# P times V in eight tensor tiles of 64 keys by 32 columns, with the halves added on GpSimd

## The chip, the cores and the metric

The kernel runs on one core of one Trainium2 chip. A core has a tensor engine (PE, with its weight loads shown as PEld), a vector engine (DVE), a scalar engine (ACT), GpSimd (POOL), and SyncE (SP), whose queue issues most of the transfers. Matrix products go into PSUM banks; the scalar and vector engines read them from there, and GpSimd works on tiles in SBUF. The metric is the device time in microseconds, the median of several executions. The profile is of one execution more.

## The reference

There are 2048 tokens of width 512, and two branches on them, mixed by a gate per token:

```
g = sigmoid((x * gate_w).sum(-1))
a = attention(x)          # 32 heads of 16, causal, window 256, softmax, then @ wo
b = mlp(layernorm(x'))    # 512 -> 1792, gelu, -> 512
out = g * a + (1 - g) * b
```

In the attention a query sees itself and the 255 keys before it:

```
mask = (i_q - i_k >= 0) & (i_q - i_k < 256)
p = softmax(where(mask, q @ k.T / 4, -1e9))
o = p @ v
```

Everything is float32 in memory.

## The kernel before, in words

There are three stages. The first makes q, k and v (lines 292, 307, 342) and the layer norm. The second holds the attention and the first MLP product side by side. The third makes the second MLP product (line 860) and the output projection (line 836).

The change touches the second stage. Its work is cut into units, and a string, `ORDER`, gives the order in which the tensor engine does them, one letter a unit:

- `S` (`s_pair`, line 368): scores of 128 queries against up to 384 keys for two heads, each head on one half of the array's rows. The vector engine takes the row maxima out of the banks (line 373).
- `T` (`st_pair`, line 412): the same scores transposed, 128 keys (block `kb`) by up to 384 queries, for two heads: `e` = 0 uses rows 0 to 63, `e` = 1 rows 64 to 113. The scalar engine takes the exponential into the tile `pts[p, kb]` (line 414), and GpSimd clears what the window excludes with one or two selects (line 416). `pts[p, kb]` holds four heads, and its 384 columns are the queries from the block's own start on.
- `f` (`fill`, line 635): one step of 24 of an MLP unit, two matmuls of 512 columns, one on each half of the rows. A unit keeps a bank pair over its 24 steps; its two banks are then copied out by the scalar engine and stored to `hp`.
- `P` (`pv`, line 431): P times V for a group `p` of four heads and 256 queries, `j`. There are 8 groups and 8 `j`, 64 units. The four heads go to the four column tiles of 32 columns (`tile_position=(0, 32 * h)`). For each head the unit has a matmul over 128 keys for each key block that its queries reach: blocks 2j - 1, 2j - 2, 2j, 2j + 1 with 256, 128, 256 and 128 queries (the two last alone where j = 0). The sums stand in one bank, 128 x 256. The scalar engine copies them (line 138) into half of an SBUF tile `acc[p]`; in the last stretch, when no S unit is left but T units are, the vector engine does (line 438). After an odd `j` the tile is stored to `osc`: by SP, one block later (line 444), or by GpSimd's own queue when all T units are out (line 446).

Scores, MLP and P times V share four bank pairs, b0 to b3, in a ring: each unit takes the one used longest ago, and an MLP unit takes one out of the ring while it runs. A bank pair can be written again when its reader is done.

A block is a T unit with `pr` = 0: `block` first calls `tick`, which runs what was put off by `after(k, ...)` until k blocks later; then it issues transfers of q and k stacks (`load_stacks`). So what stands in `after(1, ...)` is issued at the next block, ahead of that block's exponentials and selects in every engine's queue.

SBUF tiles of 128 x 512 named `t` come from a pool of nine in this stage. They serve the MLP copies (`out_half`), the raw w1 and early w2 weights, and `acc`. The early w2 loads begin at block 5 of the last group, and `attn_sums(0)`, at its block 11, is the first reader of `osc`. When the T units are out, `first_h` does the gelu and the split (line 702) of the first two tiles for the third stage, whose first matmuls (line 860) follow the last P units.

Line 138 is the helper `copy`, which is an activation on the scalar engine; line 135 is a helper that subtracts.

Of the kernel before, what the change touches and what calls it, by code (L numbers as in the profile page):

```python
# [17 lines left out]
ALU = mybir.AluOpType  # L18
# [14 lines left out]
VW = 17  # L33
# [38 lines left out]
def gated_mix_kernel(ctx, tc: tile.TileContext, xt, x2, wqk, wv, wo, xa, gw, w1, w2, b1, b2, out):  # L72
    nc = tc.nc
    dve, act, pool, pe, sp = nc.vector, nc.scalar, nc.gpsimd, nc.tensor, nc.sync
# [18 lines left out]
    def get(key, tag, bufs, shape, dt=F32):  # L93
        return left[key].tile(list(shape), dt, name=nm(tag), tag=tag, bufs=bufs)
# [3 lines left out]
    def t2(dt=F32, shape=(128, 512), tag="t"):  # L98
        return get("work", tag, BUFS.get(tag) or nt[0], shape, dt)
# [13 lines left out]
    def ps(tag, shape=(128, 512)):  # L113
        key, bufs = banks[tag]
        return left[key].tile(list(shape), F32, name=nm("ps_" + tag), tag=tag, bufs=bufs)
# [3 lines left out]
    def two():  # L119
        if not ring:  # L120
            return ps("x", (128, 2, 512))
        ring.append(ring.pop(0))
        return ps(ring[-1], (128, 2, 512))
# [13 lines left out]
    def copy(dst, src):  # L137
        act.activation(dst, src, AF.Copy)  # L138
# [3 lines left out]
    done = set()  # L142

    def after(k, fn):
        todo.setdefault(step[0] + k, []).append(fn)
# [10 lines left out]
    osc = dram.tile([8, 128, S], F32, name="osc")  # L156
# [9 lines left out]
    vs = get("ring", "v", 1, (128, NB, VR))  # L166
# [230 lines left out]
    pts, acc = {}, {}  # L397
# [21 lines left out]
    def flush():  # L419
        while late:  # L420
            late.pop(0)()

    def pv(p, j, last):
        flush()
        a = two()[:, 0]
        parts = ((-1, 0, 128, 256), (-2, 0, 256, 128), (0, 0, 0, 256), (1, 128, 0, 128))[0 if j else 2:]
        for n, (d, at, fr, w) in enumerate(parts):
            kb = 2 * j + d
            for h in range(4):
                v = (4 * p + h) * VW  # L430
                pe.matmul(a[32 * h:32 * h + 32, at:at + w], vs[:, kb, v:v + 32], pts[p, kb][:, h, fr:fr + w],  # L431
                          start=n == 0, stop=n == len(parts) - 1, skip_group_check=True, tile_position=(0, 32 * h))
        if j % 2 == 0:
            acc[p] = t2()
        s = acc[p]
        o = j % 2 * 256
        if last:
            dve.tensor_copy(s[:, o:o + 256], a[:, :256])
        else:
            copy(s[:, o:o + 256], a[:, :256])  # L440
        if j % 2:
            to = osc[p, :, (j - 1) * 256:(j + 1) * 256]
            if lt:
                after(1, lambda: sp.dma_start(to, s))
            else:
                pool.dma_start(to, s)
            done.add(("o", p, j))

    def load_consts():
        sp.dma_start(gws, view(gw, [0, 128], [1, D]))  # L450
# [275 lines left out]
    def fill():  # L726
        if cur[0] is None:
            assert {("w", *jobs[0][:2]), ("y", jobs[0][2], KT - 1)} <= done
            cur[0] = mlp1_unit(*jobs.pop(0))
        if next(cur[0], 0) == 0:  # L730
            cur[0] = None

    def block(p, kb):
        tick()
        if kb % 2 == 0:
            if kb and p + 1 < 8:
                load_stacks(p + 1, kb * 128 - 256, 256)
            if not kb and p:
                load_stacks(p, S - 256, 256)
        if p in (0, 2, 4) and kb % 2:  # L740
            double(p // 2 + 1, kb // 4, kb // 2 % 2)
        if p == 7 and kb == EB:
            early_w2()
        if p == 7 and kb == 12:
            early.extend(load_h(0, f) for f in range(2))
        if p == 7 and kb == 11:
            attn_sums(0)

    early = []
    lt = [(p, kb, pr) for p in range(8) for kb in range(NB) for pr in range(2)]  # L750
    ls = [(p, qb, pr) for p in range(8) for qb in range(NB) for pr in range(2)][2 * (NB - LAG):]
    lp = [(p, j) for p in range(8) for j in range(NB // 2)]

    def run(order):
        for a in order:
            flush()
            if a == "T":
                p, kb, pr = lt.pop(0)
                if not pr:
                    block(p, kb)  # L760
                st_pair(p, kb, pr)
                if not lt:
                    first_h()
            elif a == "S":
                s_pair(*ls.pop(0))
            elif a == "P":
                a = lp.pop(0)
                if a:
                    pv(*a, lt and not ls)
            else:  # L770
                fill()

    def first_h():
        t = spare[0]
        for f, (gelu, parts) in enumerate(early):
            gelu()
            parts((t[:, f * 2 * C:f * 2 * C + C], t[:, f * 2 * C + C:f * 2 * C + 2 * C]))

    run(ORDER)
    flush()  # L780
    run("P")
    settle()
    close_pool("work")
# [92 lines left out]
    for n in range(len(seq)):  # L876
# [10 lines left out]
        k = n + EH if n < 8 else n + 8  # L887
# [56 lines left out]
```

## Time and profile before

| | |
|---|---|
| median of 3 executions | 689.37 us (689.32 to 692.36) |
| the profiled execution | 688.0 us, of which the profile's span is 686.3 |
| tensor engine busy | 677.0 us, 99% |
| vector, scalar, GpSimd busy | 478.7, 365.4, 278.2 us |
| first and last matmul of line 431 | 156.8 and 482.9 us |
| matmuls on line 431, as the profile counts them | 1920 |

In the profile's lines, `out<-in` names the tiles written and read, `x` a count, and after the bar stand the busy time in us, the mean ns of one, and the idle time of the engine before them with what ended it. Tensor tiles are given as rows*columns. In the chain and in the timeline the first two numbers are the start and the length in us. In the waits the numbers are the total in us, the times and the longest. A float32 matmul of line 431 is run as two passes, each with its weight load, and each pass is a record.

### The profile page before, as it was taken

How to read it: one execution, taken by the hardware profiler on the slowest of the kernel's cores; microseconds unless marked ns; L12 is line 12 of the kernel's file. 1: busy time of each engine (PE TensorE's matmuls, PEld its weight loads, DVE VectorE, ACT ScalarE, POOL GpSimd, SP SyncE). 2: the span in 40 equal slices, each digit the busy share in tenths (PEclk: the TensorE clock that was granted, in tenths of full speed). 3: DMA queues.
4: the chain of work that ended last, by engine and by line, in shares of the span. 5: the costliest groups of instructions: out<-in, count | busy, mean ns of one | idle time of the engine just before them, and what ended most of it. 6: DMA issues, size and time to landing. Idle time of an engine off the chain costs nothing.

```text
span 686.3 us, 16344 instructions
## 1 busy us (share of the span) xinstructions
PE 677.0 (99%) x5738; PEld 542.4 (79%) x5738; DVE 478.7 (70%) x1491; ACT 365.4 (53%) x584; POOL 278.2 (41%) x553
## 2 busy tenths in 40 slices
PE   9999999999999999999999999999998999999997
PEld 7877777877777888787888777787877888888886
DVE  5378967797887877767868778885675654736723
ACT  5343223367776777677767678778633324214221
POOL 7210029735474655566546458558230020200300
PEclk9999999999999999999999999999999999999999
DMA  8899886886667577665685755736992551922901
GB/s 268 276 309 325 285 258 220 282 242 196 211 213 220 160 223 237 212 204 185 188 245 190 208 163 168 222 99 194 342 270 87 187 171 50 275 82 88 238 1 61
DMA packets 91590, 138.21 MB, mean 201 GB/s; under 512 B 15124, under 2 KB 38868, under 8 KB 91380
## 3 DMA queue, kind: packets, MB, share of 16 engines
q1 hardware_dynamic: 90468, 135.46, 63.0%
q8 instruction: 45, 0.74, 0.5%
q0 software_dynamic: 320, 1.05, 0.4%
q10 hardware_dynamic: 720, 0.66, 0.3%
q14 instruction: 37, 0.30, 0.1%
HBM read 81.80 MB, written 54.28 MB: 198 GB/s over the span
## 4 chain that ended last, share of the span: by engine, by line
PE 88%; DMA 8%; DVE 2%; ACT 1%; issue 1%; SPq 1%; POOL 0%; DVEq 0%; POOLq 0%; ACTq 0%
PE ps_b L635 23%; PE ps_a L860 18%; PE ps_b L431 12%; PE ps_d L307 10%; PE ps_b L412 7%; PE ps_b L368 6%; PE ps_o L836 6%; PE ps_d L342 4%; DMA or<-rd 2%; DMA t<-in_xa 2%; DMA b2s<-in_b 1%; DMA e<-hp 1%; PE ps_d L292 1%; DMA qk<-t 1%; DMA t<-in_wqk 1%; PE ps_x L368 1%
## 5 line engine op out<-in xcount | busy, mean ns | idle before, releaser
L373 DVE CUSTOM_DVE_ANT_0 scr<-ps_b,wide 128x384 bf16<-128x384 f32 (+1 forms) x472 | 227.6, 530 | 63.5 <-PE ps_b L368 61.6
L635 PE MATMUL ps_b<-x,w 64*128 64x512 f32 x1344 | 208.7, 392 | 0.7 <-DVE t L135 0.7
L416 POOL TENSOR_SCALAR_AFFINE_SELECT p<-p 128x256 f32<-128x256 f32 x368 | 140.7, 414 | 127.0 <-ACT p L414 125.6
L414 ACT ACTIVATE p<-ps_b 128x768 f32<-128x768 f32 x192 | 146.6, 795 | 30.5 <-PE ps_b L412 23.1
L860 PE MATMUL ps_a<-x,h 128*128 128x512 f32 x648 | 149.0, 389 | 0.0
L860 PEld LDWEIGHTS ps_a<-x,h 128*128 128x128 f32 x648 | 121.7, 188 | 25.2
L635 PEld LDWEIGHTS ps_b<-x,w 64*128 64x128 f32 x1344 | 128.7, 186 | 10.4 <-DVE t L135 1.1
L412 PE MATMUL ps_b<-q,k 64*128 64x384 f32 (+5 forms) x512 | 90.2, 345 | 0.2 <-DVE mx L373 0.2
L368 PE MATMUL ps_b<-k,q 62*128 62x384 f32 (+2 forms) x472 | 82.1, 336 | 0.0
L818 POOL TENSOR_TENSOR or<-or,or 128x512 f32<-128x512 f32 x16 | 22.9, 1430 | 144.2 <-DMA or<-rd 135.0
L138 ACT ACTIVATE t<-ps_b 128x256 f32<-128x256 f32 (+1 forms) x116 | 52.8, 487 | 43.5 <-PE ps_b L431 35.2
L431 PE MATMUL ps_b<-p,v 128*32 128x256 f32 (+1 forms) x1472 | 71.8, 330 | 0.0
L412 PEld LDWEIGHTS ps_b<-q,k 64*128 64x128 f32 (+1 forms) x512 | 49.2, 184 | 16.6 <-DVE mx L373 3.6
L431 PEld LDWEIGHTS ps_b<-p,v 128*32 128x32 f32 x1472 | 42.3, 110 | 23.1 <-issue 2.8
L368 PEld LDWEIGHTS ps_b<-k,q 62*128 62x128 f32 (+1 forms) x472 | 46.5, 185 | 10.1 <-issue 1.4
L416 POOL TENSOR_SCALAR_AFFINE_SELECT xq<-xq 128x256 f32<-128x256 f32 x112 | 44.3, 422 | 22.0 <-ACT xq L414 21.8
L414 ACT ACTIVATE xq<-ps_b 128x768 f32<-128x768 f32 (+1 forms) x64 | 44.2, 706 | 14.1 <-PE ps_b L412 11.7
L839 DVE SCALAR_TENSOR_TENSOR us<-b2s,g,us 128x512 f32<-128x512 f32 x16 | 12.0, 752 | 56.0 <-ACT us L838 56.0
L836 PE MATMUL ps_o<-wo,a 128*128 128x512 f32 x192 | 46.0, 390 | 2.7 <-ACT a L138 1.8
L138 ACT ACTIVATE t<-ps_d 128x512 fp32r<-128x512 f32 x32 | 19.0, 596 | 52.8 <-PE ps_d L307 45.8
L135 DVE TENSOR_TENSOR h<-e,h 128x512 fp32r<-128x512 f32 x54 | 41.0, 759 | 5.3 <-DVE h L702 0.5
L836 PEld LDWEIGHTS ps_o<-wo,a 128*128 128x128 f32 x192 | 36.0, 188 | 10.9 <-ACT a L138 2.2
(92 smaller groups left out, 754.5 us busy)
## 6 DMA issues: line engine op xcount, KB each, us to landing
qk<-t SPq DMA_DIRECT2D x72, 256.0 KB
e<-hp SPq DMA_DIRECT2D x55, 256.0 KB
hp<-t SPq DMA_DIRECT2D x54, 256.0 KB
k<-qk SPq DMA_DIRECT2D x112, 98.0 KB
q<-qk SPq DMA_DIRECT2D x112, 98.0 KB
osc<-t SPq DMA_DIRECT2D x30, 256.0 KB
w<-w SPq DMA_DIRECT2D x28, 256.0 KB
qk<-qk SPq DMA_DIRECT2D x24, 256.0 KB
```

Of the source, the lines that this page charges most:

```text
L135: eng.tensor_tensor(out=lo, in0=src, in1=f32(hi), op=ALU.subtract)
L138: act.activation(dst, src, AF.Copy)
L307: pe.matmul(o, a[:, dt * 128:(dt + 1) * 128], b[:, dt * C:(dt + 1) * C], start=n == 0, stop=n == 11)
L368: pe.matmul(o[:, e, :n], qs[pr][r:k, qb * 128:qb * 128 + 128], ks[pr][r:k, t0:t0 + n], start=True, stop=True)
L373: dve.tensor_tensor_reduce(out=sc[:, :n], in0=o[:, e, :n], in1=wide[:, 384 - n:], scale=1.0, scalar=NEG, op0=ALU.add, op1=ALU.max, accum_o ...
L412: pe.matmul(o[:, e, :w], ks[pr][r:k, kb * 128:kb * 128 + 128], qs[pr][r:k, kb * 128:kb * 128 + w], start=True, stop=True)
L414: act.activation(pt[:, :, :w], o[:, :, :w], AF.Exp, scale=0.25)
L416: pool.affine_select(out=pt[:, :, a:a + 128], in_=pt[:, :, a:a + 128], pattern=[[0, 2], [sgn, 128]], base=b, channel_multiplier=-sgn, comp ...
L431: pe.matmul(a[32 * h:32 * h + 32, at:at + w], vs[:, kb, v:v + 32], pts[p, kb][:, h, fr:fr + w], start=n == 0, stop=n == len(parts) - 1, sk ...
L635: pe.matmul(o[:, e], w[kt // 4][r:r + 64, k, m:m + 128], y[r:r + 64, a:a + C], start=n == 0, stop=n == 23)
L836: pe.matmul(a, hl[g][x][:, b * 128:b * 128 + 128], wos[g][:, k], start=n == 0, stop=n == 11)
L860: pe.matmul(accs[c][b], x[:, b * 128:(b + 1) * 128], w, start=f == 0 and n == 0, stop=f == FT - 1 and n == 2)
```

## The change

A `P` unit now works on eight tiles of 64 keys by 32 columns. The rows of a key block are taken as two halves, `r` = 0 and 1, and each half has a bank of its own in the bank pair. `parts[r]` lists, for each half, the key block (`d`), the first query column it writes (`at`) and how many (`w`). A half moves only the queries that one of its 64 keys reaches: the first half 256, 192, 128 and 64 queries of blocks 2j, 2j - 1, 2j + 1 and 2j - 2, the second half 256, 192, 128 and 64 of blocks 2j - 1, 2j, 2j - 2 and 2j + 1. For j = 0 the first half moves 256 and 128, the second 256 and 64.

The scalar engine copies both banks, 2 x 256 columns, into a `t` tile `u` of its own, always; GpSimd adds the two halves of `u` into `acc[p]`. The add is put off by one block, and the store by one more, while T units are left; after that both are issued at once.

```diff
-    def pv(p, j, last):
+    def pv(p, j):
         flush()
-        a = two()[:, 0]
-        parts = ((-1, 0, 128, 256), (-2, 0, 256, 128), (0, 0, 0, 256), (1, 128, 0, 128))[0 if j else 2:]
-        for n, (d, at, fr, w) in enumerate(parts):
-            kb = 2 * j + d
-            for h in range(4):
-                v = (4 * p + h) * VW
-                pe.matmul(a[32 * h:32 * h + 32, at:at + w], vs[:, kb, v:v + 32], pts[p, kb][:, h, fr:fr + w],
-                          start=n == 0, stop=n == len(parts) - 1, skip_group_check=True, tile_position=(0, 32 * h))
+        a = two()
+        if j:
+            parts = ((0, 0, 256), (-1, 0, 192), (1, 128, 128), (-2, 0, 64)), ((-1, 0, 256), (0, 64, 192), (-2, 0, 128), (1, 192, 64))
+        else:
+            parts = ((0, 0, 256), (1, 128, 128)), ((0, 0, 256), (1, 192, 64))
+        last = len(parts[0]) - 1
+        for n in range(last + 1):
+            for r in range(2):
+                d, at, w = parts[r][n]
+                kb, fr = 2 * j + d, at - 128 * d
+                k = slice(64 * r, 64 * r + 64)
+                for h in range(4):
+                    v = (4 * p + h) * VW
+                    pe.matmul(a[32 * h:32 * h + 32, r, at:at + w], vs[k, kb, v:v + 32], pts[p, kb][k, h, fr:fr + w],
+                              start=n == 0, stop=n == last, skip_group_check=True, tile_position=(64 * r, 32 * h))
         if j % 2 == 0:
             acc[p] = t2()
         s = acc[p]
-        o = j % 2 * 256
-        if last:
-            dve.tensor_copy(s[:, o:o + 256], a[:, :256])
+        u = t2()
+        copy(u.rearrange("p (r q) -> p r q", r=2), a[:, :, :256])
+
+        def add():
+            o = j % 2 * 256
+            pool.tensor_tensor(out=s[:, o:o + 256], in0=u[:, :256], in1=u[:, 256:], op=ALU.add)
+            if j % 2:
+                to = osc[p, :, (j - 1) * 256:(j + 1) * 256]
+                if lt:
+                    after(1, lambda: sp.dma_start(to, s))
+                else:
+                    pool.dma_start(to, s)
+                done.add(("o", p, j))
+
+        if lt:
+            after(1, add)
         else:
-            copy(s[:, o:o + 256], a[:, :256])
-        if j % 2:
-            to = osc[p, :, (j - 1) * 256:(j + 1) * 256]
-            if lt:
-                after(1, lambda: sp.dma_start(to, s))
-            else:
-                pool.dma_start(to, s)
-            done.add(("o", p, j))
+            add()
...
-                    pv(*a, lt and not ls)
+                    pv(*a)
```

## The prediction, made before the changed kernel was seen

> **What bounds the kernel now.** I read the page first (busy times, chain), then the chain in order of time around the end of the attention stage, then the groups of P times V (line 431), of the score matmuls (368, 412) and of the copies (138), and last the waits of the stretch from 156 to 483 us, where all 64 P units run.
>
> ```profile
> span 686.3 us, 16344 instructions
> PE 677.0 (99%) x5738; PEld 542.4 (79%) x5738; DVE 478.7 (70%) x1491; ACT 365.4 (53%) x584; POOL 278.2 (41%) x553
> PE 88%; DMA 8%; DVE 2%; ACT 1%; issue 1%; SPq 1%; POOL 0%; DVEq 0%; POOLq 0%; ACTq 0%
> PE ps_b L635 23%; PE ps_a L860 18%; PE ps_b L431 12%; PE ps_d L307 10%; PE ps_b L412 7%; PE ps_b L368 6%; PE ps_o L836 6%; PE ps_d L342 4%; DMA or<-rd 2%; DMA t<-in_xa 2%; DMA b2s<-in_b 1%; DMA e<-hp 1%; PE ps_d L292 1%; DMA qk<-t 1%; DMA t<-in_wqk 1%; PE ps_x L368 1%
> ```
>
> TensorE is the chain: 88% of it, 12% of the span (some 82 us) in line 431. So what the change takes from TensorE's stream in this stage comes off the end, unless something new holds TensorE up.
>
> ```profile
> core 0: us, PE busy (x) PEld busy (x) DVE busy (x) ACT busy (x) POOL busy (x), PEclk, DMA share, GB/s
> 240.00:280.00 40.00, 40.00 (x523) 31.77 (x523) 30.29 (x129) 28.43 (x46) 22.23 (x54) 1.00 0.74 230
> 440.00:483.00 43.00, 43.00 (x604) 33.76 (x600) 31.50 (x101) 32.88 (x52) 27.69 (x67) 1.00 0.52 168
> ```
>
> In the stage TensorE is never seen idle, ScalarE is at 71 to 76%, GpSimd at 56 to 64%, the clock is full.
>
> **TensorE's part.** The chain gives the price of a P unit:
>
> ```profile
> 443.04 1.44 PE ps_b L431 x32
> 444.47 0.37 PE ps_b L368 x2
> 444.84 0.17 PE ps_b L412 x2
> ...
> 450.19 2.09 PE ps_b L431 x48
> ...
> 459.04 0.23 PE ps_b L635 x2
> ...
> 467.43 4.04 PE ps_b L431 x96
> ```
>
> One unit with j over 0 is 32 records (16 calls, each run as two passes, so the 960 calls of the loops stand as 1920 records). Three of them in a row take 4.04 us and one takes 1.44, so a unit in the stream costs (4.04 - 1.44) / 2 = 1.30 us, and a unit with j = 0 costs 2.09 - 1.44 = 0.65. A column tile moves 256 + 128 + 256 + 128 = 768 columns in the first and 384 in the second: 1.693 ns per column in both, so the time goes by the moved columns alone. After the change each tile of 64 keys moves 256 + 192 + 128 + 64 = 640 columns: 1.083 us. Saved: 0.217 us in each of 56 units, 12.1 us. The eight units with j = 0 keep 256 + 128 in their longer half: nothing.
>
> That holds if eight tiles run side by side as four do. Two rows speak for it:
>
> ```profile
> 300.61 0.40 PE L431 MATMUL ps_b<-xq,v 128*32 128x128 f32 x8
> 473.19 0.34 PE L412 MATMUL ps_b<-q,k 64*128 64x384 f32 x2
> 474.92 0.34 PE L412 MATMUL ps_b<-q,k 50*128 50x384 f32 x2
> ```
>
> Eight matmuls of 128 columns, four heads by two passes, are over in 0.40 us, though the program has both passes of a head before the next head; so a column tile's second pass does not hold the others back. And the halves of the rows are independent too: a timeline row shows the form that came first, and at 474.92 the 50-row matmul, which the loop issues second, started before the 64-row one (at 473.19 it was the other way). The chain's 0.23 us for a pair of 512-column matmuls of line 635 on the two halves shows that they stream together.
>
> The eight tiles also start one after another. Of the 0.40 us, a pass of 128 columns is 0.108 and a matmul of that form lasts 0.273 (row below); the rest, 0.02 us, is three starts, some 6 ns each. Four more tiles cost 0.025 us once in each run of P units; ORDER has 49 such runs: +1.2 us. The entry and exit of a run (1.44 - 1.30 before, 0.37 against 0.17 behind: about 0.33 us, 16 us over 49 runs) I leave as they are; between 0 and all of it could go, since the rows on both sides of the change of tile then are 64 high; the nearest thing known is that it is still a change of tile shape, so I take none.
>
> The number of weight loads doubles, and the last passes are short (64 columns, 54 ns):
>
> ```profile
> L431 PEld LDWEIGHTS ps_b<-p,v x1472: 105/110/111, 156.8 to 482.3; 128*32 128x32 f32 x184
> L431 PE MATMUL ps_b<-xq,v x448: 272/273/404, 160.0 to 482.9; 128*32 128x128 f32 x86, 128*32 128x256 f32 x64
> L635 PEld LDWEIGHTS ps_b<-x,w 64*128 64x128 f32 x1344 | 128.7, 186 | 10.4 <-DVE t L135 1.1
> 478.42 0.06 PE ps_b L412 x2
> 478.48 0.28 PE ps_b L635 x2
> ```
>
> Behind a 0.06 us score pair, the next pair, whose loads last 186 ns, takes 0.28 instead of 0.23: of the load, 0.06 + 0.05 = 0.11 us is not hidden by its own latency. A 110 ns load is 76 ns shorter, which leaves 0.035 us: less than 54 ns. I take 0; the upper bound is 110 - 54 ns twice a unit, 56 times: 6.3 us.
>
> **What is added on ScalarE.** The copy out of the banks doubles, and four copies come over from VectorE:
>
> ```profile
> L138 ACT ACTIVATE t<-ps_b 128x512 f32<-128x512 f32 x56 | 30.4, 596 | 7.0 <-PE ps_b L635 6.6
> L138 ACT ACTIVATE t<-ps_b 128x256 f32<-128x256 f32 x58 | 22.3, 385 | 36.5 <-PE ps_b L431 35.2 <-ACT t L138 1.1
> L438 DVE COPY t<-ps_b 128x256 f32<-128x256 f32 x4 | 1.7, 425 | 5.2 <-POOL xq L416 2.6 <-PE ps_b L431 2.5
> ACT t L138 <- PE ps_b L431: 35.2, 47, 2.4
> PEld ps_b L431 <- ACT t L138: 3.2, 13, 0.3
> PEld ps_b L412 <- ACT t L138: 0.4, 2, 0.2
> ```
>
> Each copy goes from 385 to 596 ns, +0.21 us: 60 x 0.21 + 4 x 0.60 = 15.0 us more for ScalarE. It has the room: before 47 of the copies it sat waiting for the P unit (35.2 us). But the bank pair is free 0.21 us later, and the ring has four, one of them mostly held by the MLP unit. In 15 places TensorE's next load already waited for such a copy; each of these loses 0.21 us: 3.2 us at least. All 64 would lose 13.4 us. The exponentials behind a copy on ScalarE are later by as much and hold their own banks, and the shorter P units bring the next user sooner; so I take 4.5 us, nearer to the rows' count than to the whole.
>
> The Trainium skill warns of this: TensorEngine Tiling (Array Packing), section PSUM Bottleneck, says that tiling speeds up TensorE but not the copy out of PSUM, which may become the limit. The 35.2 us that ScalarE waits for line 431 say that it isn't the limit yet; by the page's rule taken to its end the whole 13.4 us would be paid, the second rival below.
>
> **What is added on GpSimd.** 64 adds of 128x256:
>
> ```profile
> L416 POOL TENSOR_SCALAR_AFFINE_SELECT p<-p 128x256 f32<-128x256 f32 x368 | 140.7, 414 | 127.0 <-ACT p L414 125.6
> L135 POOL TENSOR_TENSOR w<-t,w 128x512 fp32r<-128x512 f32 x12 | 15.6, 1297 | 0.5
> L516 POOL TENSOR_TENSOR t<-t,t 128x512 f32<-128x512 f32 x12 | 17.7, 1476 | 52.0 <-DMA qk<-t 51.3 <-DMA t<-in_x 0.7
> POOL p L416 <- ACT p L414: 110.6, 99, 5.2
> PEld ps_b L431 <- POOL p L416: 0.2, 1, 0.2
> ```
>
> Bounds 0.41 us (a select over as many columns) and 0.74 (half of 1476); I take half of 1297, 0.65: 42 us, in a stage in which GpSimd waits 110.6 us for exponentials. The add stands at the next block's tick, ahead of that block's selects, which wait for exponentials that ScalarE does after the copy; so it fills idle time: 0. A P unit waited for a select once, 0.2 us. The new part order wants block 2j at the unit's start and 2j + 1 at 0.76 us instead of at 0.65 and 1.08, so a few units could lose up to 0.65 us: 1 us at most, taken as 0. The spare buffer of the t ring per unit is held from the copy to the add; where three P units stand together with the early w2 loads, the nine can run out, and SP's next load waits for an add: under 1 us once, and what it loads is used blocks later. The 30 stores of osc on SP move one block on, behind the stack loads; their first reader is at block 11 of the last p. The two on GpSimd's own queue come after the last adds and are read in the last stage.
>
> **The end of the stage** moves with TensorE:
>
> ```profile
> 479.11 4.08 PE ps_b L431 x96
> 481.42 0.59 DVE L702 CAST x<-t 128x512 fp32r<-128x512 f32 x1 [3.42 <-ACT t L698]
> 482.05 0.78 DVE L135 TENSOR_TENSOR x<-t,x 128x512 fp32r<-128x512 f32 x1
> 483.08 5.74 PE L860 MATMUL ps_a<-x,x 128*128 128x512 f32 x24
> ```
>
> Line 860 starts when the last P unit is out, at 483.08; its first operand is ready at 482.01, the low part at 482.83, for the third matmul. The last three units save 0.65 us: it just fits.
>
> **The sum:** -12.1 + 1.2 + 4.5 = -6.4 us. The profiled execution took 688.0 us (span 686.3), so 681.6; the median of the runs, 689.37, is 1.4 above it, so 683.0 is what I expect of the median.
>
> **The rivals.** (B) The halves don't run side by side. If a column tile takes both halves' matmuls through one queue in program order (first half pass one, pass two, second half pass one, pass two), the second half starts one pass late, 0.216 us, and each part's first half waits for the second half's last pass of the part before to start. Worked through the four widths, the last pass starts at 1.242 us and ends at 1.296: a unit takes 1.30 as before. Nothing is saved, the 4.5 us are paid: 689.4 + 4.5 = 693.9, slower. It decides from the point at which over half of the 12.1 us is lost this way. For it: no row has eight tiles. Against it: the row at 474.92. TensorE: Matmul & The Clock Gate (Part 3, The mechanism) of the Trainium skill has matmuls start strictly in program order, which would make it this case or worse; the rows at 300.61 and 474.92 disagree. (D) Every copy is exposed: 13.4 in place of 4.5 us, 691.9, no change. For it the 15 waits that are there already, against it the 47 copies for which ScalarE was early. (C) The entry and exit of a run get cheaper, since only the tile's width changes: 6 us of the 16, 677.
>
> **Chances.** Forecast 0.57 (own range 679 to 687: the give-back between 3.2 and 8, or some of the 6.3 us of loads), C 0.13, D 0.15, B 0.15. What a measurement of this kernel can tell from no change is about 0.5%, 3.4 us. Faster by more: C and 0.48 of the forecast, 0.61; within: D and the upper end of the forecast, 0.24; slower: B, 0.15. The range goes from 676 (C) to 692 (D) and leaves out B and little else.
>
> **What would show it.** Right: runs of x64 records of line 431 spaced by 1.08 us, first pairs behind them at 0.37 again, copies of 128x512 at about 0.6 us, waits of TensorE's loads for L138 up to some 30 places, adds near 0.65 us in GpSimd's idle time. Wrong: units still 1.30 apart (B), a TensorE share in the stage below 98% with ScalarE as releaser (D), selects waited for by line 431 (GpSimd's cover gone).

## The result: slower by 1.2%

The changed kernel takes 696.87 us (median of four, 694.44 to 699.74), the kernel before 689.35 (688.38 to 692.36, with the one run added beside it): the ratio is 1.0116, with a 95% interval of 1.0085 to 1.0147. The forecast was 683.0 with a range up to 692. The profiled execution of the changed kernel took 696.1 us.

### The profile page after: what moved, and what is told of

Read it like the earlier page. It is cut to its first block, busy times and chain, and to the rows that moved or that the text cites. A ratio compares the mean times of both kernels' runs of the same rounds, so it can differ in the third digit from the quotient of the medians.

```text
span 694.3 us, 20346 instructions
## 1 busy us (share of the span) xinstructions
PE 678.2 (98%) x7658; PEld 555.9 (80%) x7658; DVE 473.9 (68%) x1487; ACT 375.9 (54%) x588; POOL 322.8 (46%) x617
## 5 line engine op out<-in xcount | busy, mean ns | idle before, releaser
L138 ACT ACTIVATE t<-ps_b 128x512 f32<-128x512 f32 x120 | 68.1, 598 | 46.4 <-PE ps_b L438 31.4
L412 PE MATMUL ps_b<-q,k 50*128 50x384 f32 (+4 forms) x512 | 92.0, 351 | 0.3 <-DVE mx L373 0.2
L438 PE MATMUL ps_b<-p,v 64*32 64x256 f32 (+3 forms) x2944 | 81.3, 303 | 6.5 <-issue 3.4
L438 PEld LDWEIGHTS ps_b<-p,v 64*32 64x32 f32 x2944 | 61.7, 105 | 25.2 <-issue 13.7
L412 PEld LDWEIGHTS ps_b<-q,k 64*128 64x128 f32 (+1 forms) x512 | 50.0, 186 | 16.3 <-ACT t L138 3.6
L448 POOL TENSOR_TENSOR t<-t 128x256 f32<-128x256 f32 x64 | 47.1, 739 | 31.3 <-ACT t L138 21.6
L368 PEld LDWEIGHTS ps_b<-k,q 62*128 62x128 f32 (+1 forms) x472 | 46.7, 185 | 13.2 <-ACT p L414 2.4
L416 POOL TENSOR_SCALAR_AFFINE_SELECT xq<-xq 128x256 f32<-128x256 f32 x112 | 42.5, 408 | 14.6 <-ACT xq L414 14.1
L851 ACT ACTIVATE us<-ps_o,g 128x512 f32<-128x512 f32 x16 | 11.0, 690 | 66.2 <-PE ps_o L849 66.2
```

The source lines that it names most:

```text
L368: pe.matmul(o[:, e, :n], qs[pr][r:k, qb * 128:qb * 128 + 128], ks[pr][r:k, t0:t0 + n], start=True, stop=True)
L412: pe.matmul(o[:, e, :w], ks[pr][r:k, kb * 128:kb * 128 + 128], qs[pr][r:k, kb * 128:kb * 128 + w], start=True, stop=True)
L416: pool.affine_select(out=pt[:, :, a:a + 128], in_=pt[:, :, a:a + 128], pattern=[[0, 2], [sgn, 128]], base=b, channel_multiplier=-sgn, comp ...
L438: pe.matmul(a[32 * h:32 * h + 32, r, at:at + w], vs[k, kb, v:v + 32], pts[p, kb][k, h, fr:fr + w], start=n == 0, stop=n == last, skip_grou ...
L448: pool.tensor_tensor(out=s[:, o:o + 256], in0=u[:, :256], in1=u[:, 256:], op=ALU.add)
```

## The profile after

First the page of the changed kernel: its span, the busy times, the queue that carries instructions, and the groups that the change touched (P times V is now line 438, the add line 448, the copy still line 138).

```profile
span 694.3 us, 20346 instructions
...
PE 678.2 (98%) x7658; PEld 555.9 (80%) x7658; DVE 473.9 (68%) x1487; ACT 375.9 (54%) x588; POOL 322.8 (46%) x617
...
q8 instruction: 61, 1.00, 0.6%
...
L138 ACT ACTIVATE t<-ps_b 128x512 f32<-128x512 f32 x120 | 68.1, 598 | 46.4 <-PE ps_b L438 31.4
...
L438 PEld LDWEIGHTS ps_b<-p,v 64*32 64x32 f32 x2944 | 61.7, 105 | 25.2 <-issue 13.7
...
L448 POOL TENSOR_TENSOR t<-t 128x256 f32<-128x256 f32 x64 | 47.1, 739 | 31.3 <-ACT t L138 21.6
```

Copies and adds cost what was expected (598 ns and 739 ns each). TensorE has 7658 matmuls and as many weight loads in its records instead of 5738. The queue q8 fetches instructions: 61 packets of 16 KB, 1.00 MB in all, some 251 matmuls and loads to a packet; before there were 45, with 255 to a packet. (The probe below shows that a packet is 256 instructions.) One wait in the row of the loads has grown: the loads of line 438 stood idle for 13.7 us with "issue" as the releaser, against 2.8 on the page of before; "issue" means that nothing in the profile held them.

Next the waits in the same kernel's stretch from 156 to 495 us (engine, line, releaser, then us in total, times, the longest in us):

```profile
PEld ps_b L438 <- issue: 13.7, 30, 2.3
...
PEld ps_b L438 <- POOL p L416: 4.6, 14, 1.0
...
PEld ps_b L412 <- ACT t L138: 3.6, 12, 0.4
PE ps_b L438 <- issue: 3.4, 3, 2.1
...
PEld ps_b L438 <- POOL t L448: 2.1, 5, 0.6
PEld ps_b L368 <- issue: 1.8, 1, 1.8
...
PE ps_b L438 <- ACT t L138: 0.8, 5, 0.2
PE ps_b L368 <- DMA q<-qk: 0.8, 1, 0.8
```

and of the waits of the kernel before, the row that answers to the first, and two of its last stage:

```profile
PEld ps_b L431 <- issue: 3.3, 12, 0.3
...
PE ps_o L836 <- ACT a L138: 1.8, 1, 1.8
...
PE ps_o L836 <- DVE a L135: 0.9, 1, 0.9
```

Twelve waits on "issue" of at most 0.3 us have become 30 of up to 2.3. They have four main places. Three are in these rows of the timeline of the changed kernel (start, duration, group, and in brackets the idle time before it); the row at 477 us is a wait for a select and not one of them:

```profile
164.00 0.57 PEld L438 LDWEIGHTS ps_b<-p,v 64*32 64x32 f32 x33 [0.98 <-issue]
...
352.24 0.44 PE L368 MATMUL ps_b<-k,q 48*128 48x384 f32 x1 [1.57 <-issue]
...
477.01 0.40 PE L438 MATMUL ps_b<-p,v 64*32 64x128 f32 x2 [0.78 <-POOL p L416]
479.46 0.55 PE L438 MATMUL ps_b<-p,v 64*32 64x128 f32 x26 [2.05 <-issue]
```

The fourth is inside the last run of three P units: 1.03 us between two neighbouring starts at 492.2 us. From start to start the four stops last 0.93, 2.01, 2.32 and 1.03 us, 6.3 us in all. Each stands inside or right behind units of line 438, in the middle of work for which the profile names nothing that was missing.

Did the eight tiles run side by side? The timeline of one undisturbed unit with j over 0 in the changed kernel says yes:

```profile
391.46 0.42 PE L438 MATMUL ps_b<-p,v 64*32 64x256 f32 x4
...
392.10 0.72 PE L438 MATMUL ps_b<-p,v 64*32 64x192 f32 x36
392.76 0.44 PE L412 MATMUL ps_b<-q,k 64*128 64x384 f32 x2
```

From its start to the next instruction the unit takes 1.30 us; before it took 1.44. So it saves 0.14 us and not the 0.19 (0.217 less 0.025) of the forecast. Between two units in a row it is much the same: mostly 1.17 us from start to start where it was 1.32 before, so 0.15 us and not 0.217. The trace shows where the rest stays. Up to the last part the starts come as the columns have it: the first matmul of 64 columns starts 1.00 us behind the unit's first, where 576 columns at 1.693 ns are 0.98. But the last part's sixteen matmuls of 64 columns start over 0.155 us or more; by an estimate from the same figures, two passes of 64 columns with eight tiles some 7 ns apart would start over 0.10. The last of them come 16 to 17 ns apart. Whether their weight loads or the pace of issue sets this was not separated. Over the stage, start to start in both traces, P units save about 6.4 us.

All 64 units compared from start to start between the two traces, the stage from the start of the first P unit to the start of the last P matmul grew from 326.1 to 336.1 us:

| part of the stage | forecast, us | measured, us |
|---|---|---|
| P units themselves | -10.9 | -6.4 |
| four stops on "issue" | 0 (bound 6.3) | +6.3 |
| later entry into P units (bank pair still being copied) | +4.5 | +3.5 |
| the same and other delays of a few ns to 0.1 us, spread over some 1100 other steps | in the above | +2.9 |
| ten steps at half the granted clock, 481.0 to 484.4 us | not seen | +1.6 |
| a select that came late in the run of three at 475 us | 0 (bound 1) | +1.0 |
| one wait for a load of q at 280 us | not seen | +1.0 |
| sum | -6.4 | +9.9 (of 10.0) |

Two rows need a word. Fourteen of the fifteen P units that were entered over 0.15 us later than before have their first matmul 0.14 us behind the end of a copy (line 138), so the copy is the wait. The loads' rows in the waits above name GpSimd's selects and adds, but in twelve of these fourteen places those had been done for 0.6 to 2.4 us.

And a stop can have a second price. The mean granted clock from the third stop to the fourth (third number from the end) is not full:

```profile
479.40:493.20 13.80, 13.07 (x253) 11.10 (x254) 4.97 (x9) 11.89 (x19) 9.04 (x22) 0.88 0.46 158
```

In the trace it is 0.50 from 481.0 to 484.4 us and 1.00 on both sides, and ten steps there, f and T units that the change left alone, take 1.6 us longer than before. The kernel before has no such stretch in this stage. The second profile of the changed kernel has two, of 3.4 us each, behind its second and third stop (353 and 483 us), with 1.65 and 1.56 us. That the stop brings the half clock on is read from its place; no run tests it.

The span grew by 8.0 us only: the stage began 1.0 us later, and the part behind the last P matmul took 200.4 instead of 203.4 us, since the wait of the last stage's matmuls of line 836 (1.8 + 0.9 us in the rows above) did not occur. The second profiles below show how much of that is chance.

## The experiments

Theory I (instructions): TensorE's instructions, doubled in the P units, do not arrive in time. Theory R (ring): the longer copies, two banks and the adds eat the gain. All ratios are against the kernel before, run on the same chip beside it.

### Halves without eight tiles (x1_halves)

Each P matmul of the kernel before becomes two of half the columns. Columns, banks, copies stay; the instructions of the P units double.

```
-            for h in range(4):
-                pe.matmul(a[..., at:at + w], vs[...], pts[p, kb][:, h, fr:fr + w], ...)
+            m = w // 2
+            for i in range(2):
+                for h in range(4):
+                    pe.matmul(a[..., at + i * m:at + i * m + m], vs[...], pts[p, kb][:, h, fr + i * m:fr + i * m + m], ...)
```

> The kernel before, with every matmul of P times V cut into two of half the columns. The columns moved, the copies and everything else are as before; only the matmuls and weight loads of a unit double, to the number that the changed kernel has (64 pairs for j over 0). Theory I (TensorE's instructions come late: a sequencer rate of some 8 ns an instruction, and stalls of 1 to 3 us without any releaser in long runs of P units): slower than before by 5 to 9 us, with stalls named issue of some 8 us in sum in the stage. Theory R (the loss is in the copies, the ring of banks and the adds): as before, within 1 us, no such stalls.

Measured: 695.51 us against 688.95, ratio 1.0099 (1.0065 to 1.0134). Its waits:

```profile
PEld ps_b L433 <- issue: 7.2, 15, 1.6
PEld ps_b L433 <- ACT t L138: 3.3, 13, 0.3
PE ps_b L433 <- issue: 3.4, 3, 1.4
```

What follows: four tiles, one bank and one copy, and yet 6.6 us slower. An undisturbed unit lasts 0.02 us longer than before (1.31 us from its first start to its last and 0.15 us to the next instruction, before 1.24 and 0.20), so the shorter pieces cost some 1 us in all. The stage is 7.6 us longer: three stops make 4.0 of it, and two waits of S units near 260 us, which the rows put down to a load of q and to the maxima, another 1.4. Theory R, which saw nothing here, falls as the only cause, and theory I stands.

### Two copies without eight tiles (x2_copies)

The four tiles of before, but two of the four key blocks go to a second bank; both banks are copied, GpSimd adds.

```
-            pe.matmul(a[..., at:at + w], ..., start=n == 0, ...)
+            pe.matmul(a[..., r, at:at + w], ..., start=n in (0, 2), ...)
...
-        copy(s[:, o:o + 256], a[:, :256])
+        copy(u.rearrange("p (r q) -> p r q", r=2), a[:, :, :256])
+        pool.tensor_tensor(out=s[:, o:o + 256], in0=u[:, :256], in1=u[:, 256:], op=ALU.add)
```

> The kernel before, with four tiles of 128 keys and the same number of matmuls, but the parts of blocks 2j - 1 and 2j - 2 go to the first bank and those of 2j and 2j + 1 to the second, both are copied out and GpSimd adds them one block later, as in the changed kernel (for j = 0 one bank and one copy, as before). So the copies and adds alone, on 56 units. Theory I: slower than before by 3 to 5 us, all of it waits for banks. Theory R: slower by 10 us or more, enough to eat the 12 us that the shorter streams should save and the 7.5 that the change lost.

Measured: 693.93 us, ratio 1.0057 (1.0020 to 1.0095). Its waits for the copy:

```profile
PEld ps_b L433 <- ACT t L138: 4.8, 14, 0.4
PEld ps_b L412 <- ACT t L138: 2.6, 9, 0.4
PEld ps_b L368 <- ACT t L138: 1.2, 5, 0.3
```

Before, these were 3.2, 0.4 and nothing (13, 2 and no places). So the copies' price is 8.6 - 3.6 = 5.0 us by these rows and 3.5 us from start to start in the P stage, where one wait for a load of q (1.1 us at 276 us, here too) is left out. The forecast of 4.5 us lies between the two. Both causes are real, and neither alone is the 7.5 us.

### One bank without the second copy (x3_onebank)

The changed kernel, but only the first bank is copied, and nothing is added: the second half of the keys is left out of the output.

> The changed kernel with its eight tiles, but only the first half's bank is copied out, 256 columns, by the engine that did it before, and nothing is added; the second half of the keys is left out of the sums that are stored. So the change without the copies and adds. Theory I: 4 to 5 us faster than the changed kernel, about 692, still not faster than before; stalls named issue remain. Theory R: 12 us faster than the changed kernel or more, 683 to 685.

Measured: 694.04 us, ratio 1.0066 (1.0031 to 1.0101). The stops stay:

```profile
PEld ps_b L438 <- issue: 14.5, 34, 2.4
PE ps_b L438 <- issue: 4.7, 5, 2.2
```

In 33 groups of neighbouring P units, each compared from start to start with the kernel before, 26 are faster here, by up to 0.4 us, and the seven others, in which the stops stand, are slower by 0.1 to 2.4 us. (This trace is of the slowest of nine executions, 697.78 us.) In the changed kernel itself the 29 groups without a stop or a late load lie between -0.22 and +0.44 us and come to +0.4 us together. So without the stops, the copies and waits for banks give back what the shorter stream brings: that is the second half of the answer.

### Quarters (x4_quarters)

As x1_halves with four pieces.

> As the halved one, but cut into four: 128 pairs of load and matmul in a unit with j over 0, the same columns. Theory I: a pair is issued each 16.6 ns, so a unit takes 128 x 16.6 ns = 2.1 us in the stream in place of 1.30, and the kernel is slower by 45 us or more. Theory R: as before, within 1 us.

Measured in one run: 783.65 us, 95 us more.

```profile
PEld ps_b L433 <- issue: 59.6, 45, 4.5
PE ps_b L433 <- issue: 51.3, 31, 4.4
```

That is twice what theory I gave, because an undisturbed unit is not the loss: it lasts 1.45 us from first to last start and 1.47 to the next unit's start (256 instructions, 5.7 ns each), only 0.14 us more than with halves. The stops are. In the three runs of three units, 768 instructions took 9.0, 11.6 and 10.7 us. So in the main it is not the pace of issue, but the supply that runs out.

### Which units (x5_runs, x6_others)

Halves only in the nine units that stand three in a row (LONG = 34 to 36 and 58 to 63), and only in the others:

```
+            c = 2 if 8 * p + j in LONG else 1      # x6_others: not in LONG
+            m = w // c
```

> The four tiles of before, with every P matmul cut in two column halves only in the nine P units that stand three in a row in the order (units 34 to 36 and 58 to 63); the other units as before. If runs of P outrun the supply of TensorE instructions (theory I), the loss of the kernel with halves everywhere sits to more than half in these nine units: its two last runs of three lasted 5.61 and 5.52 us where those of before last 3.84, so +2.5 to +4 us here, with waits on 'issue' only at these runs. If the loss goes with the number of added instructions wherever they stand (theory N), nine of 60 units' worth carry 15% of 6.6 us: +1.0 us.

> The complement: halves in all P units but those nine. Theory I: +1.5 to +3.5 us, from places where one or two P units follow close on other dense stretches. Theory N: +5.6 us.

Measured: 691.58 us, ratio 1.0043 (1.0021 to 1.0064), and 692.77 us, ratio 1.0063 (1.0037 to 1.0089), beside 688.27 before. In microseconds 3.0 and 4.3. The first lies where theory I had it and above N (1.0); the second lies between I (1.5 to 3.5) and N (5.6) and fits neither. Nine units carry 40% of the loss, but "three in a row" is not the condition.

### Four tiles in the long runs, split copies (y4_mixed, y2_split)

y4_mixed takes the changed kernel and gives the same nine units the four tiles, one bank and one copy of before. y2_split lets VectorE copy the second bank:

```
-        copy(u.rearrange("p (r q) -> p r q", r=2), a[:, :, :256])
+        copy(u[:, :256], a[:, 0, :256])
+        dve.tensor_copy(u[:, 256:], a[:, 1, :256])
```

> The changed kernel, but the nine P units that stand three in a row keep the four tiles, one bank and one copy of before. Theory I: the waits on 'issue' at 350, 475 and 489 us go (1.85 + 3.46 + 1.07 us), and 9 x 0.14 us of stream saving go with them: 696.9 - 6.4 + 1.2 = 691.7 us, still above before by the ring's waits and by two smaller waits on 'issue'. If the loss comes from the copies, the bank ring and the adds (theory R), only 9 of 64 units are spared and the time falls by about 1 us, to 696.

> The changed kernel with ScalarE copying one bank and VectorE the other (256 columns each) in place of one ScalarE copy of 596 ns; GpSimd adds as before. If the waits for a P's pair of banks (3.5 us) come from the length of the copy, they mostly go: 693 to 695 us. If VectorE, which has the maxima of the S units in its queue, takes its copy late, a wait of the same size stands at the same places: 696 to 699 us.

Measured: y4_mixed 694.78 us, ratio 1.0092 (1.0066 to 1.0119). The stops in the long runs are gone, but two others have come (1.30 us at 248 us, 0.76 at 414) and the first has grown from 0.93 to 1.47 us, so some 2 us of the expected 5 were gained. y2_split 708.62 us, ratio 1.0280 (1.0227 to 1.0334), far outside of both expectations. Its group of VectorE's copies from 200 to 460 us, and the waits of TensorE's loads for them:

```profile
L445 DVE COPY t<-ps_b 128x256 f32<-128x256 f32 x44 | 18.4, 419 | 17.5 <-ACT t L138 15.4 <-issue 1.6 <-DMA hp<-t 0.3
```

```profile
PEld ps_b L412 <- DVE t L445: 7.4, 18, 0.6
...
PEld ps_b L368 <- DVE t L445: 5.8, 13, 0.8
```

VectorE's copy of 419 ns waited for ScalarE's (15.4 us in all; both write the tile `u`), so the two copies often ran one after the other, and TensorE's loads waited 13.2 us for the second. The run says nothing on copies that run side by side.

### Number, order, choice of units (x7_fhalves, y0_order, y1_spread, y7_clean)

x7_fhalves leaves the P units alone and halves the matmuls of the f units (512 columns to two of 256). y0_order and y1_spread break the three runs of three apart with neighbouring f units (SSPPPST becomes SSPffPffPST, and so on), in the kernel before and in the changed one. y7_clean gives eight tiles to 21 units only, chosen as those around which the changed kernel had shown no stop and no wait for a bank; the last run of three (units 61 to 63) is among them all the same, though the fourth stop, at 492 us, stands in its last unit.

> The kernel before, with the P units untouched and every matmul of the f units (first MLP multiplication, 512 columns) cut in two of 256: about 2700 more TensorE instructions at places where an instruction lasts long, against 3840 more in the kernel with halves in P. Theory I (only dense stretches outrun the supply): within 1 us of before, no waits on 'issue' at P. Theory N (the loss goes with the number of instructions): 2700/3840 x 6.6 = +4.6 us. An f unit that itself gets longer than 231 ns would show as such in its start to start.

> The kernel before with the three runs of three P broken up by f units that stood next to them (same units, same number of each). Six more runs at an entry and exit of 0.33 us each: 688.3 + 2.0 = 690.3 us. It is the control for the next.

> The changed kernel with the same order. Theory I: the 6.4 us of waits on 'issue' at the three long runs go, and six more entries and exits come (2.0 us): 692.5 us, 2 us above the control. Theory N, or a loss from the copies: the loss against the control stays 7 to 8 us, so 697 to 699 us.

> The four tiles of before, but the eight tiles in the 21 units around which the profile of the changed kernel showed no wait for a bank and no wait on 'issue'. By what these places saved in the profile (0.05 to 0.22 us each): 1.5 to 2.5 us below before, 686 to 687 us, if instructions come in time elsewhere too. If late instructions appear wherever there are more of them, 689 us or more.

Measured, beside 687.91 us before: x7_fhalves 695.03, ratio 1.0102 (1.0065 to 1.0140); y0_order 691.33, ratio 1.0057 (1.0038 to 1.0076); y1_spread 699.01, ratio 1.0149 (1.0121 to 1.0178); y7_clean 688.67, ratio 1.0004 (0.9985 to 1.0024).

x7_fhalves looks like theory N, but its trace has not one stop: each f unit itself is 5.5 ns longer from start to start, 3.7 us over 672 of them, and the part behind the P stage 2.3 us longer by a wait of the last stage. Some 2700 more instructions where one lasts long ran out nowhere. y1_spread refutes theory I as it was put: against its control it loses as much as the changed kernel does (7.7 us). Within the P stage the loss falls from 10.0 to 5.6 us, but three stops remain, of which only one (at 479 us) is near a broken run and one (at 226 us) is new; the rest of the difference lies behind the P stage (202.9 against 200.8 us). And y7_clean kept one stop, in that last run (at 482 us):

```profile
PEld ps_b L439 <- issue: 4.1, 7, 2.2
```

### The supply by itself, and what repeats (z1_probe, after_b, before_b, y9_fewer)

z1_probe is the kernel before with 512 tiny matmuls behind the last P unit:

```
+    a = two()
+    for n in range(512):
+        r, h = n % 2, n // 2 % 4
+        pe.matmul(a[32 * h:32 * h + 32, r, :32], vs[64 * r:64 * r + 64, 0, :32], vs[64 * r:64 * r + 64, 0, 32:64], ...)
...
```

after_b and before_b are the two kernels once more; y9_fewer is y7_clean without the last three units.

> The kernel before with 512 small matmuls (eight tiles of 64 keys by 32 columns in turn, 32 columns moved, result unused) behind the last P unit: with both fp32 passes and their weight loads 2048 TensorE instructions of almost no work. It measures the supply by itself. Theory I, with the rate that the kernel with quarters showed in its runs of three (768 instructions in 9.0 to 11.6 us, so 11.8 to 15 ns each): 24 to 31 us, in stretches of fast issue with waits on 'issue' of 1 to 3 us between them, about one per 256 instructions. If instructions always come in time and the sequencer's own rate is the limit (12.5 ns a pair of load and matmul in an undisturbed unit of the kernel with quarters): 13 us without gaps.

> The changed kernel once more, for a second profile. Theory I: waits on 'issue' of 6 to 10 us again, at the run of three near 473 us and at two to four of the other dense places, though not all the same ones, since a fetch that comes late by chance decides. A cause fixed in the code would show the same places with the same sizes. The part behind the last P unit, 200.4 us in the first profile of this kernel and 203.4 in that of before, tells whether that difference belongs to the kernel.

> The kernel before once more, for a second profile. If the 3 us more behind the last P unit are chance of the execution, they may be gone here; if they belong to the kernel, 203 us again. From first to last P unit 326 us as before.

> The kernel with eight tiles only in the clean units, now without the last three in a row (units 61 to 63), where the profile of that kernel showed a wait on 'issue' of 2.2 us: 18 units with eight tiles, the others with four. Its units saved 0.05 to 0.17 us each in that profile, 1.1 us in all: 0.998 of before, at the edge of what can be told; 1.000 or more if late instructions find another place.

The timeline of the probe, and then its loads' waits:

```profile
492.00 1.42 PEld L786 LDWEIGHTS ps_b<-v 64*32 64x32 f32 x128 [2.58 <-issue]
492.00 1.55 PE L786 MATMUL ps_b<-v 64*32 64x32 f32 x128 [2.45 <-issue]
495.73 1.42 PEld L786 LDWEIGHTS ps_b<-v 64*32 64x32 f32 x128 [2.31 <-issue]
```

```profile
PEld ps_b L786 <- issue: 19.6, 8, 3.4
```

The 2048 instructions took 30.7 us, at the upper end of what theory I gave (24 to 31), and more than twice the other (13). The rows show how: 128 loads and 128 matmuls run in 1.4 us, then TensorE's loads stand still, eight times in all, for 3.4 us at first and for 2.0 to 2.6 us after that, and TensorE mostly goes on every 3.7 us. One block of 256 instructions, one packet of 16 KB. Nor is it traffic that delays these packets, since hardly any other is there. The transfers from 484 to 515 us (packets, MB, share of the 16 engines), and one block of the same stretch (busy time of each engine, then granted clock, DMA share and GB/s):

```profile
q8 instruction: 8, 0.13, 1.9%
```

```profile
495.70:499.40 3.70, 1.55 (x128) 1.42 (x128) 0.00 (x0) 0.00 (x0) 0.00 (x0) 0.50 0.02 4
```

Eight packets, one for each block; and during a block the DMA engines are 2% busy. (The granted clock had fallen to 0.50 there, so the 1.4 us are not at full speed.)

This gave the question that explained all earlier runs: at which instruction does TensorE stop? Counted over all of its records in each trace (matmuls, weight loads and its sequencer's), every gap of over 0.7 us between two starts from 155 to 590 us falls in one of two classes. Those at one count, 193 above a multiple of 256:

```
kernel            stops at 193 mod 256   us together   where (us from the span's start)
before, before_b  0                      0
x2, x7, y0        0                      0
after             4                      6.3           163  350  477  492
after_b           4                      6.8           163  351  480  495
x1_halves         3                      4.0           273  479  493
x3_onebank        5                      8.8
x4_quarters       34                     67.1
x5 / x6           3 / 2                  4.5 / 1.8
y4 / y1           3 / 3                  3.5 / 4.1
y2                4                      5.8
y7 / y9           1 / 0                  2.2 / 0
z1_probe          8                      20.4          (one after each 256)
```

All others are waits for a load of q (0.7 to 1.7 us, at 259 to 281 us; why the load comes late in some kernels stays open), for a select, for banks, or in the last stage; none of those of the changed kernel is put down to "issue" by the profile. In the four stops of the changed kernel, TensorE went on 1.40, 1.41, 1.51 and 1.36 us after an instruction packet on q8 had ended; in all stops of the table it is 1.2 to 1.6 us.

The same packets show what else a stop hangs on. In these four, the packet began 3.44, 1.53, 1.88 and 1.15 us after TensorE had passed the limit before, and it took 1.13, 1.55, 2.55 and 0.96 us; in the probe it mostly began 1.0 to 1.7 us after the limit and took 0.9 to 1.4. So the work in a block does not decide alone: the first stop stands behind a block of 5.05 us of work, whose packet began late, and the third behind 3.62 us, with the packet that took longest, while a block of 3.31 us (at 243 us) passed without a stop. Whether the transfers around a packet make it late or long was not tested.

after_b has the same four places as the first profile with sizes within 0.3 us, so the place is in the code, not chance. What theory I had expected, places that change, was wrong.

The part behind the last P unit was 203.2 us in before_b (203.4 in the first profile), but 205.3 in after_b against 200.4:

```profile
PE ps_o L849 <- ACT a L138: 2.7, 1, 2.7
```

This wait is there or not by the execution, and after_b took 703.43 us. Single profiles are to be compared within the P stage, not over the span.

y9_fewer: 687.27 us beside 688.18, ratio 0.9987 (0.9964 to 1.0010), with no stop at 193 in its trace; a late load of q cost 1.7 us there (at 274 us).

### The block limits moved (y8_shift, y10_clean_shift)

The last two change only where the blocks of 256 begin in the program's work: 160 more TensorE instructions at the very start of the changed kernel, and 208 (`SHIFT = 53`) at that of y7_clean.

```
-WARM = 10
+WARM = 8
+SHIFT = 41
...
+        for n in range(SHIFT):
+            h = n % 4 * 32
+            pe.matmul(o[h:h + 32, :32], f32(blank)[:64, :32], f32(blank)[:64, :32], ...)
```

> The changed kernel with 160 more TensorE instructions at its very start (two of the ten warm-up matmuls out, 41 tiny ones in), so that each block of 256 instructions begins 160 instructions earlier in the program's work. The waits on 'issue' of the changed kernel all stand at the same count of instructions modulo 256 (193), and the probe's too. If a block that is worked off sooner than the next can arrive makes the wait (theory I, now with its place), the sum over blocks of what lacks to 3.6 us falls from 2.8 to 0.3 us by this shift, and the four waits of 0.9, 2.0, 2.3 and 1.0 us go: 696.9 - 6.3 = 690.6 us, with the waits for banks left. If the waits come at dense places whatever the block (or from the traffic there), they stay: 695 to 699 us.

> The kernel with eight tiles in the 21 clean units (y7_clean), shifted by 208 instructions in the same way, where its one wait on 'issue' (2.2 us in the last run of three) should go: 688.7 - 2.2 = 686.5 us, 0.997 to 0.998 of before. If the block's place does not matter, 688.7 us again.

Measured: y8_shift 698.94 us beside 689.67, ratio 1.0139 (1.0112 to 1.0166); y10_clean_shift 689.62, ratio 1.0003 (0.9986 to 1.0021). The waits of y8_shift's loads, and one row of its timeline:

```profile
PEld ps_b L443 <- issue: 11.8, 27, 1.9
...
PEld ps_o L854 <- ACT a L139: 3.1, 1, 3.1
```

```profile
443.28 0.15 PEld L443 LDWEIGHTS ps_b<-p,v 64*32 64x32 f32 x8 [1.91 <-issue]
```

The mechanism held and the sum did not. All four stops left their places: the work at 163, 350, 477 and 492 us of the changed kernel runs through here. But three others stand at the new limits, 273, 330 and 441 us (1.64, 1.23 and 1.96 us), again at 193 modulo 256. The stage from first to last P unit fell by 3.2 us, to 332.9, and the last stage's wait took more than that back. The estimate of 0.3 us counted a block as safe that is worked off in 3.6 us; the three stops stand behind blocks of 3.45, 3.59 and 3.41 us, whose next packet began 2.92, 2.45 and 3.01 us after the limit. What makes the fetch of one block start later than that of another was not found. y10_clean_shift did not gain what was expected: its P stage has no stop left and is 1.1 us shorter than that of before, but a stop of 1.36 us stands just behind it, at 483 us in the first matmuls of the last stage, again at 193.

None of the versions beats the kernel before: y9_fewer, the best, is within what can be told from no change.

## Why the prediction was wrong

**That eight tiles run side by side** was right, and rival B, which denied it, wrong: 1.30 us for a unit and what follows instead of 1.44. The size was off: the stream saves 6.4 us, not 12.1 - 1.2. The term "cost by columns" held up to the last part of a unit; there the sixteen short matmuls start over 0.155 us or more instead of 0.10, in each of 56 units.

**The step that failed is the doubled instructions.** The prediction looked at the weight loads' duration, found that a load of 110 ns hides, and took 0 with a bound of 6.3 us. With four tiles the duration does hide, all but 0.02 us a unit: x1_halves has twice the loads and takes 1.46 us from a unit's first start to the next instruction, where 1.44 were taken before. What the prediction didn't ask is whether the instructions are there. The four stops cost 6.3 us in the first profile and 6.8 in the second, and the half clock behind them another 1.6 and 3.2; that the bound has the size of the stops is chance. Without them the change would have been no change, with them it is slower. The stage was to be 6.4 us shorter and was 9.9 us longer: of these 16.3 us the stops and the clock are 7.9, the smaller saving 4.5, the copies and small delays 1.9, the late select and the late load of q 1.0 each.

**The copies** were forecast at 4.5 us; x2_copies alone shows 3.5 to 5.0. In the changed kernel the entries into P units cost 3.5, and small delays in other steps another 2.9, of which x2_copies shows 2.1; what the rest is was not separated.

**The adds** run 739 ns (0.65 taken, bound 0.74) and are hidden but for a select that came late once (1.0 us in the run of three at 475 us), as the bound of 1 us had it. **The entry and exit of a run** got a little cheaper (0.15 instead of 0.20 us behind the last start), far from rival C. **Rivals B and D**, 693.9 and 691.9, came nearest in time, but for wrong reasons: the tiles do run side by side, and the copies cost about what was forecast and not 13.4 us. **The end of the stage** moved along with TensorE, as said, but the last stage's wait for scaled rows, of up to 3 us by the execution, hides or doubles what a single profile shows.

No rival had this mechanism, though the page of before held half of it: 45 packets of 16 KB on q8 for 11476 matmuls and loads are 255 each, and the chain has a run of three units, 192 instructions in 4.04 us. Doubled, a block is done in under 3 us. What the page doesn't hold is that the next block can take longer than that to come; the probe showed it, with 3.7 us.

## What to carry to other kernels

Splitting a TensorE step into more tiles multiplies its instructions; count them per microsecond at the densest place, not over the kernel. In the probe 256 instructions came every 3.7 us (14 to 15 ns each). In the kernels with two pieces or eight tiles, stops of 0.8 to 2.6 us stood at the limits of blocks with 2.4 to 5.1 us of work, with nothing on record but "issue"; most limits passed without one. Where such stops appear, count the instructions between them before looking for a semaphore, and weigh the second bank's copy against the saved columns: here the two were about equal.

## What the runs showed of the hardware that was not expected

TensorE's instructions arrive in packets of 16 KB, 256 each. In the probe, 256 instructions of almost no work ran in 1.4 us, at a granted clock of 0.50, and the next came 3.7 us after the ones before, with 2% of the DMA engines busy. The Trainium skill, page "Runtime: NRT & Kernel Launch", section "Instruction fetch mechanics", has the fetch mostly hidden because an engine's sequencer is slower than the refill; these runs disagree, with waits of up to 4.5 us in x4_quarters, and 5.7 ns for an instruction in its undisturbed units.

Halving or quartering the moved columns of a matmul cost little by itself (1.24 us from a unit's first start to its last before, 1.31 with two pieces, 1.45 with four), as long as instructions were there. And a mean over executions hides a wait that is there or not: the last stage waited 0 or 3 us in profiles of one and the same kernel.
